# Softmax steps on an even grid of stages, one staging copy per product, and token steps and loads in other places

## The chip, the cores and the metric

The kernel runs on one core of a Trainium2 chip. The metric is device time in microseconds (us), from launch to end. The engines of the core are named as the profile names them: PE (TensorE, matrix products and transposes), DVE (VectorE), ACT (ScalarE), POOL (GpSimd) and SP (SyncE, which issues the DMAs here). Each engine works through its own instructions in the order in which they were written.

## The reference

The program chains three layers over 8 batches of 8 heads, 576 positions and a head width of 64. Keys and values are averaged over groups of 8 positions (72 pooled positions per head), attention is taken over these, and its result, as 4608 tokens of width 512, goes through two feed-forward networks:

```
k_p, v_p = mean of 8 neighbouring positions of k, v
a = softmax(q @ k_p.T / 8) @ v_p            # per batch and head
x = a as (4608, 512)
x = leaky_relu(x @ w_in) @ w_out            # 512 -> 2048 -> 512
xn = x / rms(x) * g
out = (silu(xn @ w_gate) * (xn @ w_val)) @ w_out2   # 512 -> 1536 -> 512
```

All of it is computed to fp32 precision: most operands are split into a high and a low part, and a product takes three matmuls.

## The kernel before

The tokens go through the first network in blocks of 512, j = 0 to 8. Blocks 0 to 4 are computed plainly; blocks 5 to 8 go in two pairs (q = 0, 1) by a scheme with fewer products, and the second network follows in pairs too.

**Stages.** In a plain block PE's work is cut into stages of six matmuls. For each f the order is: two halves of h (`h_half`, product with w_in), then two parts of y for f - 2 (`y_unit`, product with w_out). After the second half of h, `h_high` issues two ACT passes (L101) and `h_low` one DVE subtraction (L619), which make the operand for y. After each stage `attention_point` is called, which issues whatever was put at this point's number. Point 28 is the first of block 1, 92, 156 and 220 are the first of blocks 2, 3 and 4.

**Attention in between.** Attention of batches 0 and 1 is done inside block 0, in an order written out by hand. From batch 2 on `late_attention` puts it at points. A tile is 128 queries of a batch (five tiles, t = 0 to 4; tile number i = 5 b + t, from 10 to 39). `start[i]` is the point at which tile i begins. Its steps are generators, called once per listed point:

- `step_s`: first scores of four heads (PE, L322) and their maximum and subtraction (DVE, L335, L336), then the same for the other four heads one point later, the exponential (ACT, L341) at s + 3, and the normalisation (four DVE instructions, L343 to L346) at s + 4.
- `step_r`: two ACT copies of the leftover columns (L374).
- `step_x`: four transposes on PE (L383), the high part on ACT (L387), the low part on DVE (L389). `step_y` does the same for the leftover columns (L397, L401, L404).
- `step_t`: transposes of the next tile's q (L302) and an ACT copy (L308). `step_kt`: transposes of the next batch's pooled keys and four or eight ACT copies (L294).
- `step_av`: the product with v (four matmuls, L426 and L431). For tokens of blocks 0 to 4 it goes on as high part (ACT, L445) and low part (DVE, L459); for blocks 5 to 8 ACT copies it to a staging tile (L452), which two points later SP stores to DRAM (L454).

Scores, transposes and products of the late batches share two PSUM banks (`bank("att", 2, ...)`), which go round in the order of issue: what takes a bank waits until the one before the last has been read.

**Around the pairs.** In block 4 `first_pair` puts loads and token steps of pair 0 at stage numbers of that block (`put(i, x)` runs ahead of that stage's `attention_point`). Token steps (`token_steps`) make the sums and splits of the pair's inputs on DVE (L1074, L98), ACT and POOL. In the pairs' output stage pieces of six matmuls (L1343) are issued one after another; in the loop over them the loads of the next pair's inputs and the token steps are called at given piece numbers i.

Of the kernel before, what the change touches and what calls it, by code (L numbers as in the profile page):

```python
# [9 lines left out]
F32 = mybir.dt.float32  # L10
# [13 lines left out]
def pooled_attention_then_two_ffns(  # L24
# [13 lines left out]
    nc = tc.nc  # L38
    B, H, S, D = q.shape
    queries = q  # L40
    NT, DM = out.shape
    P = 128
# [9 lines left out]
    N = 512  # L52
# [7 lines left out]
    CHMAX = 320  # L60
# [6 lines left out]
    per = ctx.enter_context(tc.tile_pool(name="per", bufs=1))  # L67
# [12 lines left out]
    def scratch(b, name, early=False):  # L80

        return bank("att", 2, name) if b else bank("ya" if early else "yb", 2, name)
# [21 lines left out]
    def cols(w, f):  # L104
        return w[:, f * W:(f + 1) * W].rearrange("(c p) f -> p c f", p=P)

    def rows(w, f):
        return w[f * P:(f + 1) * P, :]
# [58 lines left out]
    ap = att.__enter__()  # L167
# [5 lines left out]
    for h, sign in ((0, -1), (1, 1)):  # L173
        nc.gpsimd.affine_select(
            out=mask_main[:, h:h + 1], in_=mask_main[:, h:h + 1], compare_op=ALU.is_ge, fill=0.0,
# [4 lines left out]
    for sign, base in ((1, 0), (-1, REST - 1)):  # L180
        nc.gpsimd.affine_select(
            out=group, in_=group, compare_op=ALU.is_ge, fill=0.0, base=base, channel_multiplier=sign,
# [4 lines left out]
        out=mask_rest[:, :, 1], in_=group.rearrange("p d q -> p q d"), axis=AX.X, op=ALU.add  # L187
# [223 lines left out]
    def x_tile(j):  # L411
        if j not in xhl:
            if j == 3:
                xhl[j] = [weight_slot(9 + 2 * c, f"xhl{j}_{c}") for c in range(KC)]
            else:
                t = per.tile([P, 2, KC, N], F32R, tag="xhl", bufs=2, name=f"xhl{j}")
                xhl[j] = [t[:, :, c, :] for c in range(KC)]
        return xhl[j]

    def step_av(b, ci, p):  # L420
        c0, c1, _ = CH[ci]
        n = c1 - c0
        a, ar = at[b, ci]
        pt = scratch(b, f"av{b}_{ci}_{p}")
        for i, (sp, mp) in enumerate(TERMS):
            nc.tensor.matmul(  # L426
                pt[:, :n], vb[b, p][:, sp].rearrange("p h d -> p (h d)"), a[:, p, mp, 0:n],
                start=i == 0, stop=False,
            )
        g, i = divmod(p, 2)  # L430
        nc.tensor.matmul(  # L431
            pt[:, :n], vb[b, NP + g][:, 2 * i:2 * i + 2, :].rearrange("p h d -> p (h d)"), ar[:, g, 0:n],
            start=False, stop=True,
        )
        yield
        spans = []
        t0 = b * S + c0
        while t0 < b * S + c1:
            j = t0 // N
            t1 = min((j + 1) * N, b * S + c1)  # L440
            src = pt[:, t0 - b * S - c0:t1 - b * S - c0]
            if j < PLAIN:
                x = x_tile(j)[p][:, :, t0 - j * N:t1 - j * N]
                spans.append((x, src))
                nc.scalar.activation(out=x[:, HI, :], in_=src, func=AF.Copy)  # L445
            else:
                name = f"xs{b}_{ci}_{p}_{j}"
                if p < 2:
                    x = ap.tile([P, CHMAX], F32, tag="xs", bufs=2, name=name)[:, :t1 - t0]
                else:  # L450
                    x = per.tile([P, N], F32, tag="tg", bufs=3, name=name)[:, :t1 - t0]
                nc.scalar.copy(out=x, in_=src)  # L452
                def store(x=x, j=j, a=t0 - j * N, z=t1 - j * N):
                    nc.sync.dma_start(out=x_dram[j][:, p, a:z], in_=x)  # L454
                at_point.setdefault(point_now[0] + 2, []).append(store)
            t0 = t1
        yield
        for x, src in spans:
            nc.vector.tensor_tensor(out=x[:, LO, :], in0=src, in1=x[:, HI, :].bitcast(F32), op=ALU.subtract)  # L459

    tiles = [(b, t) for b in range(B) for t in range(5)]
# [8 lines left out]
    def go(kind, b, t):  # L470
        if (kind, b, t) not in running:
            running[kind, b, t] = emit[kind](b, t)
        if running[kind, b, t] is not None:
            next(running[kind, b, t], None)
# [33 lines left out]
    def late_attention():  # L508

        def put(point, f):  # L510
            at_point.setdefault(point, []).append(f)

        def stage(kind, b, t, points):
            for point in points:
                put(point, lambda: go(kind, b, t))
            if kind in use:
                def free():
                    live["q" if kind == "t" else "kv"] -= 1
                put(points[0] + 3, free)

        start = {}
        for i in range(FIRST_LATE, len(tiles) + 1):
            start[i] = 34 + round(7.9 * (i - 10))
        for r, point in enumerate((4, 9, 14, 29, 31)):
            stage("kp", 2, r, (point,))
        stage("kt", 2, 0, (28,) * 2)
        stage("kt", 2, 1, (34,) * 2)
        stage("t", 2, 0, (28,) * 2)
        for i in range(FIRST_LATE, len(tiles)):
            b, t = tiles[i]  # L530
            s, after = start[i], start[i + 1]
            stage("s", b, t, (s, s, s + 1, s + 1, s + 3, s + 4))
            stage("r", b, t, (s + 6,))
            stage("x", b, t, (s + 7,) * 3)
            stage("y", b, t, (s + 8,) * 3)
            if i + 1 < len(tiles):
                stage("t", *tiles[i + 1], (s + 6,) * 2)
            if t < 2:
                for k in range(3):
                    stage("vp", b, 3 * t + k, (s + 2 * k,) * 2 + (s + 2 * k + 2,) * 2)  # L540
            if t in (2, 3) and b + 1 < B:
                for k in range(3 if t == 2 else 2):
                    stage("kp", b + 1, 3 * (t - 2) + k, (s + 4 * (t - 2) + 2 * k,))
                stage("kt", b + 1, t - 2, (after + 3,) * 2)
            if t in (1, 4):
                for p in range(NP):
                    stage(f"av{t // 4}", b, p, (after + 2 + p,) * 3)

    point_now = [0]
    first_left = {"V1l5", "T14c"}  # L550
# [27 lines left out]
    for at_, (m, f) in enumerate(needs):  # L578
        src = rows(w_out, f) if m == "o" else cols(w_in, f)
        n = 2 * f + (m == "o")  # L580
# [365 lines left out]
    pairs, kinds = [], []  # L946
# [31 lines left out]
    def pair_loads(q):  # L978

        n = pairs[q][1]  # L980
        xs = [[None] * KC for _ in range(2)]

        def load(z, k):
            x = slot("u", (6, 7, 2, 3)[2 * z + k] if q else 8 + 2 * z + k, f"xst{q}_{z}_{k}").bitcast(F32)
            j = pairs[q][0] // N + z
            nc.sync.dma_start(out=x, in_=x_dram[j][:, 2 * k:2 * k + 2, :])
            for c in range(2):
                xs[z][2 * k + c] = x[:, c, :]

        return xs, [lambda z=z, k=k: load(z, k) for z in range(2) for k in range(2)]  # L990
# [205 lines left out]
    def first_pair(put):  # L1196

        xs, loads = pair_loads(0)
        early, late = token_steps(0, xs, True)
        for i, x in zip((14, 15, 18, 19), loads):  # L1200
            put(i, x)
        for i, x in zip((25, 27, 29, 31, 33, 36, 38, 41), early):
            put(i, x)
        for i, x in zip((58, 59), late):
            put(i, x)
        for i in (34, 36, 39, 41, 42, 44, 46, 48, 50, 52):
            put(i, load_a)
        for i in (53, 55, 57, 59):
            put(i, load_o)
# [260 lines left out]
    n = 0  # L1470
# [10 lines left out]
    for j in range(1, PLAIN):  # L1481
# [3 lines left out]
        def put(i, x):  # L1485
            at_spot.setdefault(i, []).append(x)
# [10 lines left out]
        if last:  # L1497
            first_pair(put)
# [22 lines left out]
    def piece():  # L1521
        if pieces:
            pieces.pop(0)()
# [16 lines left out]
    def tick():  # L1540
        for x in late_side.pop(0) if late_side else ():
            x()

    for q, (_, n) in enumerate(pairs):
# [3 lines left out]
        loads, xs, norm = [], None, []  # L1548
        if more:
            xs, steps = (pair_loads if kinds[q + 1] == 1 else norm_steps)(q + 1)  # L1550
            if kinds[q + 1] == 1:
                loads = steps
# [72 lines left out]
        early, late = token_steps(q + 1, xs, kinds[q] == 1) if more else ([], [])  # L1625
# [11 lines left out]

        for i in range(len(pieces) - (4 if more else 0)):
            if kinds[q] == 1:
                if loads and i in (0, 1, 4, 8):  # L1640
                    loads.pop(0)()
                piece()
                if early + late and (i >= 12 if kinds[q + 1] == 1 else i >= 4 and i % 2 == 0):
                    (early or late).pop(0)()
                for k in (4, 5) if i == 3 else (i // 2 + 4,) if i % 2 and i > 3 else ():
                    if k < F1:
                        second_half(q, k)
                tick()
                continue
            if i % 3 == 0 and early + late:  # L1650
                (early or late).pop(0)()
            piece()
# [42 lines left out]
```

## Time and profile before

| | |
|---|---|
| median of 3 runs | 1814.41 us (1814.34 to 1816.33) |
| profiled execution | 1814.61 us |
| its span, first to last instruction | 1812.9 us |
| PE busy | 1748.3 us, 96% |
| DVE, ACT, POOL busy | 937.2, 720.8, 650.6 us |
| mean granted clock of PE | 0.991 |

The span is counted from the first instruction to the last. Busy time of PE contains modelled ends of matmuls. In a list of waits, `PE sc L322 <- DVE at L389` reads: PE, about to write the tile sc at line 322, stood still until DVE had finished the instruction of line 389 on the tile at. In a timeline a row gives start, duration, engine, line and operation, the tiles, the shapes, and in brackets how long the engine was idle before and what ended that.

### The profile page before, as it was taken

The numbers are of one execution on the slowest core, as the hardware profiler recorded it, in microseconds if no ns is written. First come the engines' busy times: TensorE is split into PE (matmuls) and PEld (weight loads), VectorE is DVE, ScalarE is ACT, GpSimd is POOL, SyncE is SP. The second block draws the span as 40 slices with busy tenths as digits, with TensorE's granted clock in tenths as the row PEclk, the third lists the DMA queues.
The fourth block names the chain that finished last, engine by engine and source line by source line (L and its number), as shares of the span: only waits on it lengthen the run. The fifth ranks groups of instructions, "written<-read, shape, count | busy, mean of one in ns | idle before, by whom it ended". The sixth has DMA issues, their size and how long they took to land.

```text
span 1812.9 us, 24130 instructions
## 1 busy us (share of the span) xinstructions
PE 1748.3 (96%) x8440; PEld 1480.3 (82%) x8440; DVE 937.2 (52%) x1633; ACT 720.8 (40%) x1539; POOL 650.6 (36%) x797
## 2 busy tenths in 40 slices
PE   5899999999999899989999999999999999999999
PEld 4789877777887788867888888899788889988887
DVE  7984445656565454565755345344534444553331
ACT  5664344444454344444553432243232323322220
POOL 5632335535433023443443442154144204513320
PEclk9899999999999999999999999999999999999999
DMA  8543654546666579879996755786775568776562
GB/s 247 191 149 109 231 194 150 162 146 203 192 201 203 165 269 329 302 281 360 313 311 209 238 204 204 227 305 242 247 255 185 188 223 321 253 252 214 187 209 93
DMA packets 214729, 406.36 MB, mean 224 GB/s; under 512 B 58704, under 2 KB 116560, under 8 KB 214096
## 3 DMA queue, kind: packets, MB, share of 16 engines
q1 hardware_dynamic: 214608, 404.82, 66.2%
q8 instruction: 67, 1.10, 0.2%
q14 instruction: 54, 0.44, 0.1%
HBM read 328.21 MB, written 76.55 MB: 223 GB/s over the span
## 4 chain that ended last, share of the span: by engine, by line
PE 79%; DVE 7%; DMA 5%; ACT 3%; issue 3%; POOL 1%; SPq 1%; POOLq 0%; ACTq 0%; DVEq 0%
PE o L1363 16%; PE h L596 8%; PE y L641 8%; PE o L1343 7%; PE yg L1235 6%; PE yv L1235 6%; PE xg L1235 4%; PE xv L1235 4%; PE wg L1235 4%; PE wv L1235 4%; PE yh L1235 3%; PE wh L1235 2%; DMA v<-in_v_dram 2%; PE xh L1235 2%; PE sc L322 2%
## 5 line engine op out<-in xcount | busy, mean ns | idle before, releaser
L1363 PE MATMUL o<-wo,u 128*128 128x512 f32 x1296 | 316.5, 392 | 3.8 <-DMA wo<-wo 3.7
L1363 PEld LDWEIGHTS o<-wo,u 128*128 128x128 f32 x1296 | 243.3, 189 | 53.4 <-DMA wo<-wo 4.7
L596 PE MATMUL h<-xhl,w_i 128*128 128x512 f32 (+1 forms) x996 | 249.9, 393 | 6.9 <-DVE ghl L619 5.5
L596 PEld LDWEIGHTS h<-xhl,w_i 128*128 128x128 f32 x996 | 176.9, 190 | 37.6 <-DVE ghl L619 6.0
L641 PE MATMUL y<-ghl,w_o 128*128 128x256 f32 (+1 forms) x768 | 151.7, 344 | 0.0
L98 POOL TENSOR_TENSOR u<-e2g,u 128x512 fp32r<-128x512 f32 (+1 forms) x25 | 29.6, 1185 | 312.4 <-ACT u L95 312.4
L641 PEld LDWEIGHTS y<-ghl,w_o 128*128 128x128 f32 x768 | 118.7, 192 | 13.2
L619 DVE TENSOR_TENSOR ghl<-h,ghl 128x512 fp32r<-128x512 f32 (+1 forms) x83 | 55.6, 670 | 124.5 <-ACT h L101 124.5
L641 PE MATMUL y<-ghl,wr 128*128 128x512 f32 x384 | 101.8, 405 | 0.0
L1343 PE MATMUL o<-ug,wo 128*128 128x512 f32 x384 | 92.4, 399 | 6.0 <-DMA wo<-wo 3.8
L1343 PE MATMUL o<-u,wo 128*128 128x512 f32 x384 | 96.2, 389 | 0.0
L1343 PEld LDWEIGHTS o<-ug,wo 128*128 128x128 f32 x384 | 73.7, 193 | 23.0 <-issue 4.2
L101 ACT ACTIVATE ghl<-h 128x512 fp32r<-128x512 f32 (+1 forms) x83 | 48.3, 582 | 99.6 <-PE h L596 93.7
L1343 PEld LDWEIGHTS o<-u,wo 128*128 128x128 f32 x384 | 72.1, 188 | 14.9
L1235 PE MATMUL yg<-T,ag 128*128 128x512 f32 (+1 forms) x360 | 84.0, 368 | 0.0
L1235 PE MATMUL yv<-T,av 128*128 128x512 f32 (+1 forms) x360 | 83.8, 368 | 0.0
L1235 PE MATMUL xg<-xa,ag 128*128 128x512 f32 (+1 forms) x360 | 83.8, 367 | 0.0
L1235 PE MATMUL xv<-xa,av 128*128 128x512 f32 (+1 forms) x360 | 83.7, 367 | 0.0
L641 PEld LDWEIGHTS y<-ghl,wr 128*128 128x128 f32 x384 | 70.9, 193 | 12.8
L322 PE MATMUL sc<-kblk,qT 128*128 128x144 f32 x320 | 60.0, 316 | 15.5 <-DVE at L389 9.9
L1235 PEld LDWEIGHTS yg<-T,ag 128*128 128x128 f32 x360 | 66.0, 188 | 10.0 <-DVE e1v L1212 0.6
L1235 PEld LDWEIGHTS yv<-T,av 128*128 128x128 f32 x360 | 66.2, 188 | 9.5
(204 smaller groups left out, 3450.5 us busy)
## 6 DMA issues: line engine op xcount, KB each, us to landing
wo<-wo SPq DMA_DIRECT2D x172, 512.0 KB
ag<-op_g SPq DMA_DIRECT2D x90, 512.0 KB
av<-op_v SPq DMA_DIRECT2D x90, 512.0 KB
wr<-wo SPq DMA_DIRECT2D x32, 512.0 KB
ah<-op_h SPq DMA_DIRECT2D x32, 512.0 KB
k<-in_k_dram SPq DMA_DIRECT2D x40, 256.0 KB
q<-in_q_dram SPq DMA_DIRECT2D x40, 256.0 KB
op_g<-parts_g SPq DMA_DIRECT2D x36, 256.0 KB
```

What stands on the lines that cost most here:

```text
L98: lo_eng.tensor_tensor(out=lo, in0=src, in1=hi.bitcast(F32), op=ALU.subtract)
L101: return nc.scalar.activation(out=out, in_=in_, func=AF.Prelu, scale=scale, alpha=alpha)
L322: nc.tensor.matmul(pt[:, i * n:(i + 1) * n], y[:, p, :], kblk[b % 2][:, p * n:(p + 1) * n], start=True, stop=True,)
L596: nc.tensor.matmul(pt, w[:, sp, c * P:(c + 1) * P], x[c][:, mp, c0:c1], start=c == 0 and i == 0, stop=c == KC - 1 and i == 2,)
L619: nc.vector.tensor_tensor(out=t[:, LO, :], in0=pt, in1=t[:, HI, :].bitcast(F32), op=ALU.subtract)
L641: nc.tensor.matmul(pt, w[:, sp, m * P:(m + 1) * P], g[:, mp, a - c0:a - c0 + n], start=ydone[j, a] == 1 and i == 0 and m % per_bank == 0, ...
L1235: nc.tensor.matmul(pt, wt[:, a, c, sp, :], xt[:, mp, :], start=start and c == 0 and i == 0, stop=c == 1 and i == 2, skip_group_check=not s ...
L1343: nc.tensor.matmul(pt, w[:, sp, m * P:(m + 1) * P], u[:, mp, :], start=f == blocks(q, z)[0] and i == 0, stop=f == blocks(q, z)[-1] and i == 2,
L1363: nc.tensor.matmul(pt, u[:, sp, m * P:(m + 1) * P], w[:, mp, :], start=f == 0 and i == 0, stop=f == F2 - 1 and i == 2,)
```

## The change

- `start[i]` is 33 + 8 (i - 10) in place of 34 + round(7.9 (i - 10)): from 33 to 265 for the tiles, where it was 34 to 263.
- `step_r`, `step_x`, `step_y` and the next tile's `step_t` stand one point sooner after a tile's start, and the products with v one point sooner after its end. Two of batch 2's key steps and one of its transposes move with the first start.
- `step_av` makes one staging copy for a product that crosses two blocks of 512 tokens, and two stores of parts of it, in place of two copies and two stores.
- In block 4 the pair's token steps stand at stages 20 to 46 in place of 25 to 41, and two of its loads a stage sooner.
- In pair 0's output stage the four loads of the next pair's inputs stand at pieces 6, 9, 12 and 15 in place of 0, 1, 4 and 8, and its token steps begin after piece 16 in place of 12.

```diff
-                name = f"xs{b}_{ci}_{p}_{j}"
-                if p < 2:
-                    x = ap.tile([P, CHMAX], F32, tag="xs", bufs=2, name=name)[:, :t1 - t0]
-                else:
-                    x = per.tile([P, N], F32, tag="tg", bufs=3, name=name)[:, :t1 - t0]
-                nc.scalar.copy(out=x, in_=src)
-                def store(x=x, j=j, a=t0 - j * N, z=t1 - j * N):
+                if t0 == b * S + c0:
+                    name = f"xs{b}_{ci}_{p}"
+                    if p < 2:
+                        whole = ap.tile([P, CHMAX], F32, tag="xs", bufs=2, name=name)
+                    else:
+                        whole = per.tile([P, N], F32, tag="tg", bufs=3, name=name)
+                    nc.scalar.copy(out=whole[:, :n], in_=pt[:, :n])
+                def store(x=whole[:, t0 - b * S - c0:t1 - b * S - c0], j=j, a=t0 - j * N, z=t1 - j * N):
...
-            start[i] = 34 + round(7.9 * (i - 10))
-        for r, point in enumerate((4, 9, 14, 29, 31)):
+            start[i] = 33 + 8 * (i - 10)
+        for r, point in enumerate((4, 9, 14, 28, 30)):
...
-        stage("kt", 2, 1, (34,) * 2)
+        stage("kt", 2, 1, (32,) * 2)
...
-            stage("r", b, t, (s + 6,))
-            stage("x", b, t, (s + 7,) * 3)
-            stage("y", b, t, (s + 8,) * 3)
+            stage("r", b, t, (s + 5,))
+            stage("x", b, t, (s + 6,) * 3)
+            stage("y", b, t, (s + 7,) * 3)
             if i + 1 < len(tiles):
-                stage("t", *tiles[i + 1], (s + 6,) * 2)
+                stage("t", *tiles[i + 1], (s + 5,) * 2)
...
-                    stage(f"av{t // 4}", b, p, (after + 2 + p,) * 3)
+                    stage(f"av{t // 4}", b, p, (after + 1 + p,) * 3)
...
-        for i, x in zip((14, 15, 18, 19), loads):
+        for i, x in zip((14, 15, 17, 18), loads):
...
-        for i, x in zip((25, 27, 29, 31, 33, 36, 38, 41), early):
+        for i, x in zip((20, 22, 25, 29, 34, 38, 42, 46), early):
...
-                if loads and i in (0, 1, 4, 8):
+                if loads and i in (6, 9, 12, 15):
...
-                if early + late and (i >= 12 if kinds[q + 1] == 1 else i >= 4 and i % 2 == 0):
+                if early + late and (i >= 16 if kinds[q + 1] == 1 else i >= 4 and i % 2 == 0):
```

From the staging copy on (L452 of before), lines carry a number higher by one in the changed kernel.

Three places show what moves. The first is DVE in tile 0 of batch 6, from its last scores to behind its normalisation; `ghl3_11` is the low part of h for block 3, f = 11. Before:

```order
L336 TENSOR_TENSOR ex6_0_5087<-sc6_0_1_5108,st6_0_5088 128x288
L741 TENSOR_TENSOR raw_g0_0_4939<-raw_g0_0_4939 128x128 x4
L274 TENSOR_TENSOR vb6_0_5134<-vm6_0_5095,vb6_0_5134 128x128
L343 TENSOR_REDUCE st6_0_5088<-ex6_0_5087 128x8
L344 TENSOR_TENSOR st6_0_5088<-st6_0_5088,tiny_67 128x8
L345 RECIPROCAL st6_0_5088<-st6_0_5088 128x8
L346 TENSOR_TENSOR ex6_0_5087<-ex6_0_5087,st6_0_5088 128x576
L274 TENSOR_TENSOR vb6_1_5182<-vm6_1_5141,vb6_1_5182 128x128
L619 TENSOR_TENSOR ghl3_11_0_5200<-h3_11_0_5162,ghl3_11_0_5200 128x512
```

The changed kernel, the same stretch of DVE:

```order
L336 TENSOR_TENSOR ex6_0_5090<-sc6_0_1_5121,st6_0_5091 128x288
L274 TENSOR_TENSOR vb6_0_5139<-vm6_0_5098,vb6_0_5139 128x128
L620 TENSOR_TENSOR ghl3_11_0_5179<-h3_11_0_5151,ghl3_11_0_5179 128x512
L343 TENSOR_REDUCE st6_0_5091<-ex6_0_5090 128x8
L344 TENSOR_TENSOR st6_0_5091<-st6_0_5091,tiny_67 128x8
L345 RECIPROCAL st6_0_5091<-st6_0_5091 128x8
L346 TENSOR_TENSOR ex6_0_5090<-ex6_0_5090,st6_0_5091 128x576
```

The low part of h stood behind the normalisation and now stands ahead of it.

The second place is PE in the same tile, from the second half of h (f = 11) to the transposes of the normalised scores (`xt6_0`). The changed kernel:

```order
L597 MATMUL h3_11_0_5151<-xhl3_3_2772,w_i11_1157 128x512 x3
L426 MATMUL av5_1_3_5183<-at5_1_4800,vb5_3_4542 128x320 x3
L431 MATMUL av5_1_3_5183<-atr5_1_4801,vb5_5_4625 128x320
L642 MATMUL y3_0_0_4518<-ghl3_9_0_5023,wr3_9_4953 128x512 x3
L642 MATMUL y3_0_1_4519<-ghl3_9_0_5023,wr3_9_4953 128x512 x3
L302 MATMUL qt6_1_5216<-ident_63,q6_1_4979 128x128 x4
L642 MATMUL y3_0_2_4520<-ghl3_9_0_5023,wr3_9_4953 128x512 x3
L642 MATMUL y3_0_3_4521<-ghl3_9_0_5023,wr3_9_4953 128x512 x3
L383 MATMUL xt6_0_5236<-ident_63,ex6_0_5090 128x128 x4
```

In this tile PE's rows stand as before, two parts of y between that h and the transposes; what DVE does beside them is in the other order. In a tile that started after a second half of h before, half a further h stood between them too.

The third place is PE at the start of the same tile, from the first scores to the second. Before:

```order
L322 MATMUL sc6_0_0_5084<-kblk0_72,qT6_0_5053 128x144 x2
L596 MATMUL h3_10_0_5070<-xhl3_2_2790,w_i10_1064 128x512 x3
L596 MATMUL h3_10_0_5070<-xhl3_3_2791,w_i10_1064 128x512 x3
L322 MATMUL sc6_0_1_5108<-kblk0_72,qT6_0_5053 128x144 x2
L641 MATMUL y3_0_0_4523<-ghl3_8_0_4983,wr3_8_4895 128x512 x3
```

The changed kernel:

```order
L322 MATMUL sc6_0_0_5087<-kblk0_72,qT6_0_5045 128x144 x2
L642 MATMUL y3_0_0_4518<-ghl3_8_0_4968,wr3_8_4874 128x512 x3
L642 MATMUL y3_0_1_4519<-ghl3_8_0_4968,wr3_8_4874 128x512 x3
L426 MATMUL av5_1_0_5114<-at5_1_4800,vb5_0_4350 128x320 x3
L431 MATMUL av5_1_0_5114<-atr5_1_4801,vb5_4_4583 128x320
L322 MATMUL sc6_0_1_5121<-kblk0_72,qT6_0_5045 128x144 x2
```

A product with v now takes one of the two banks between the first scores and the second.

## Rows read from the trace of the kernel before

**Rows 1.** The page's busy times: us (share of the span) and instructions

```profile
PE 1748.3 (96%) x8440; PEld 1480.3 (82%) x8440; DVE 937.2 (52%) x1633; ACT 720.8 (40%) x1539; POOL 650.6 (36%) x797
```

**Rows 2.** Busy by stretch: us, engines PE PEld DVE ACT POOL, clock, DMA share, GB/s

```profile
176.00:264.00 88.00, 85.95 (x438) 71.37 (x437) 41.53 (x91) 35.79 (x97) 25.62 (x54) 1.00 0.61 219
264.00:400.00 136.00, 128.94 (x648) 104.92 (x647) 79.01 (x180) 58.61 (x150) 67.99 (x111) 0.99 0.53 164
400.00:545.00 145.00, 142.51 (x736) 118.40 (x735) 84.18 (x181) 72.63 (x192) 65.01 (x116) 1.00 0.61 191
545.00:615.00 70.00, 63.44 (x319) 52.31 (x319) 41.35 (x77) 30.00 (x72) 18.35 (x30) 0.98 0.62 194
```

**Rows 3.** PE's waits from 190 to 615 us: total, times, longest

```profile
PE sc L322 <- DVE at L389: 9.4, 12, 2.7
PE xt L383 <- ACT xs L452: 3.1, 2, 2.8
```

**Rows 4.** Busy by stretch again, at the lower clock, columns as in rows 2

```profile
356.80:360.20 3.40, 2.97 (x9) 2.59 (x10) 3.27 (x8) 0.63 (x1) 3.20 (x7) 0.50 0.60 162
...
776.60:783.40 6.80, 5.74 (x14) 4.53 (x15) 0.00 (x0) 0.18 (x1) 1.83 (x4) 0.50 1.04 411
```

**Rows 5.** Timeline near 350 us, tile 1 of batch 4: start, us, engine, line

```profile
349.08 0.69 DVE L619 TENSOR_TENSOR ghl<-h,ghl 128x512 fp32r<-128x512 f32 x1 [3.10 <-ACT h L101]
...
350.84 1.64 PE L596 MATMUL h<-xhl,w_i 128*128 128x512 f32 x6
350.91 0.76 DVE L346 TENSOR_TENSOR ex<-ex,st 128x576 f32<-128x576 f32 x1
```

**Rows 6.** Timeline near 385 us, tile 3 of batch 4, with next batch's keys

```profile
384.23 1.64 PE L596 MATMUL h<-xhl,w_i 128*128 128x512 f32 x6
...
385.04 1.94 POOL L762 TENSOR_TENSOR hr<-w_i 128x256 f32<-128x256 f32 x2
...
385.38 1.02 DVE L346 TENSOR_TENSOR ex<-ex,st 128x576 f32<-128x576 f32 x1
...
386.55 0.63 PE L383 MATMUL xt<-ident,ex 128*128 128x128 f32 x4 [0.68 <-DVE ex L346]
```

**Rows 7.** Timeline from 325 to 338 us, tile 0 of batch 4, with products

```profile
325.28 1.65 PE L641 MATMUL y<-ghl,wr 128*128 128x512 f32 x6
...
327.51 0.46 DVE L336 TENSOR_TENSOR ex<-sc,st 128x288 f32<-128x288 f32 x1
...
331.00 0.60 PE L426 MATMUL av<-at,vb 128*128 128x320 f32 x3
...
336.57 0.76 DVE L346 TENSOR_TENSOR ex<-ex,st 128x576 f32<-128x576 f32 x1
...
337.25 1.64 PE L596 MATMUL h<-xhl,w_i 128*128 128x512 f32 x6
```

**Rows 8.** First pair's output stage: a stretch, a wait of PE, and timeline rows

```profile
760.00:825.00 65.00, 56.46 (x233) 45.01 (x232) 43.25 (x60) 28.48 (x59) 34.19 (x32) 0.95 0.78 273
...
PE yh L1235 <- DVE e6h L1212: 2.6, 1, 2.6
...
765.76 8.09 PE L1343 MATMUL o<-ug,wo 128*128 128x512 f32 x35
...
768.42 0.60 SPq L986 DMA_DIRECT2D xst<-x  x1
...
770.12 1.16 SPq L1186 DMA_DIRECT2D wo<-wo  x2
...
777.66 6.59 PE L1343 MATMUL o<-ug,wo 128*128 128x512 f32 x16 [3.80 <-DMA wo<-wo]
...
787.35 1.37 DVE L98 TENSOR_TENSOR xa<-xst,xa 128x512 fp32r<-128x512 f32 x1 [1.64 <-ACT xa L95]
...
818.01 0.68 DVE L1212 TENSOR_TENSOR e6h<-yh,e1h 128x512 f32<-128x512 f32 x1
```

**Rows 9.** Timeline: one of the token steps' three subtractions in block 4

```profile
580.99 0.68 DVE L1074 TENSOR_TENSOR T<-xst,xst 128x512 f32<-128x512 f32 x1
```

## Prediction

> **What bounds the kernel now.** I read the page first: the line of busy times says that TensorE (PE) works 96% of a span of 1812.9 us, and no other engine more than 52% [rows 1]. So PE is the path, and only two things can change the time: microseconds in which PE stands still, and microseconds in which it has half its clock. Next I cut the part where the change acts into four stretches [rows 2]. From 176 to 615 us (the softmax steps of batches 2 to 7) PE stands still for 2.05 + 7.06 + 2.49 + 6.56 = 18.2 us. Then the list of waits, PE only, for the same part: half of it is scores waiting for the VectorE (DVE) instruction that frees their bank (`sc <- DVE at`, 12 times, longest 2.7), 3.1 is transposes behind ScalarE (ACT) staging copies, longest 2.8 [rows 3]. Behind the longest of each kind a stretch of 3.4 us ran at a granted clock of 0.50, the lower of the two levels (1.2 of 2.4 GHz); the means of 0.99 and 0.98 in rows 2 hold one each. In the one shown PE was busy 2.97 us, half of which is lost: 1.5, so 3.0 in the two [rows 4]. Later PE waits in the first pair's output stage: from 760 to 825 us it stands still 65 - 56.46 = 8.5 us, 3.8 of it at once for weights, and 6.8 us run at the lower clock, 5.74 of them busy, so 2.9 lost [rows 4, 8].
>
> **Part 1, the softmax steps.** Before, a tile starts every 7.9 stages, rounded, so its place against the four-stage pattern (two halves of h, two of y) drifts: tiles 10 to 15 start after the first y, 16 to 24 after the second half of h, 25 to 35 after the first half, 36 to 39 after the second y. In the changed kernel all 30 tiles start after a second half of h (33 + 8k), so tiles 16 to 24 of before stand already where all will stand, and can be measured there.
>
> *What goes.* The four transposes now stand two stages ahead of the next tile's scores and the small transposes one, so the scores no longer find their bank unread. I count all 18.2 us and the 3.0 us of clock as gone and put what comes in their place on the other side.
>
> *What comes, first: the transposes wait for the normalisation.* Four stages after a tile's start, a second half of h has just been computed. DVE takes its instructions in order, and in this place the low part of that h (L619) stands ahead of the normalisation (L343 to L346), as the order in front shows. It can't start until PE has finished h and ACT has done two passes on it. A tile without products, at 346 us, shows the chain: L619 waits for ACT until 349.08 and ends at 349.77, and L346 ends at 350.91 + 0.76 = 351.67 [rows 5]. The stage to which the transposes move (after the second y) ended at 350.84, where the next h starts in that row. Reading the operand took 0.15 us after L346's end elsewhere (386.55 against 385.38 + 1.02) [rows 6]. So PE waits 351.82 - 350.84 = 1.0 us. The one stage of h that the transposes are moved past was the cover, and nothing else is left to cover with; behind them in PE's queue is all further matmul work.
> - Tiles t=1: as this, 1.0 each, six of them: 6.0.
> - Tiles t=3 of five batches: eight ACT copies of the next keys stand ahead of the two passes. L346 ends at 386.40, and the place of the transposes is 384.23: 2.3 us [rows 6]. L346 took 1.02 there instead of 0.76; I take 2.0, five: 10.0.
> - Tiles t=4 with four such copies: estimated between the two, 1.3, five: 6.5.
> - Tiles t=0 and t=2 with products and their DVE low parts (five): L346 ends at 336.57 + 0.76 = 337.33, h starts at 337.25, and one product of 0.60, which now comes ahead of that stage, no longer stands in between: 337.48 - 336.65 = 0.8 each, 4.0 [rows 7]. From batch 4's second half on the products leave no low part on DVE (about 0.4 less): six tiles by 0.3: 1.8. The remaining three without copies or products by 1.0: 3.0.
> Sum 31.3. In the tile at stage 241 the first pair's three subtractions, moved to stage 245, land on DVE between L619 and the normalisation: three by 0.68, 2.1 more with what lies between them [rows 9]. With that 33.4.
>
> *What comes, second: the second scores wait for the first.* Products move a stage sooner, so one takes a bank between the two halves of the scores, and the two banks go round: the second scores now need the bank of the first, which L336 must have read. In the tile at 325 us L336 ends at 327.51 + 0.46 = 327.97, or a little sooner, since the small low part ahead of it (L404) moves away. PE starts y at 325.28; y takes 1.4 (six matmuls at 35 in 8.09 us), the product 0.6, and the small transposes that stood before them are gone, so PE is there by 327.1 [rows 7, 8]: I take 0.8, in eleven tiles (t=0 from batch 3, t=2): 8.8.
>
> These bounds: a wait of the transposes is at least 0.5 and at most 2.6 (2.3 with the longest chain, plus a little); the sum from 24 to 40. The second scores from 0.4 to 1.0: 4 to 11.
>
> *Clock.* Waits of 2.7 and 2.8 us brought a stretch at half clock [rows 3, 4]; one of 2.6 didn't: the mean clock of 0.95 from 760 to 825 us is explained by the 6.8 us behind the wait for weights alone (6.8 by 0.5 of 65 is 0.05) [rows 4, 8]. Of the new waits only the one with the subtractions (3.1) is above: 1.5.
>
> Softmax part: 33.4 + 8.8 + 1.5 - 18.2 - 3.0 = +22.5 us.
>
> **Part 2, one staging copy.** Twelve 256-column copies replace 24 pieces of batches 5, 6 and 7, whose second piece waited for a store to free its slot. Its gain on PE is the 3.1 us of transposes behind `xs` [rows 3], in the 18.2 already; ACT itself has room (40%) [rows 1]. If the single copies should still wait, up to 3.1 comes back, and the 1.5 of clock behind the longest.
>
> **Part 3, first pair's token steps in the last block.** The same instructions on ACT and DVE, over more stages; cost nothing but the 2.1 above. Loads a stage earlier: what they read was stored some 20 stages before. The last products and their stores come a stage later than before, with PE on its own last four h and y stages: 0, bounded by -1 and +2.
>
> **Part 4, the loads in the first pair's output stage.** Three loads of 512 KB were issued from 768.42 on, around the two weight loads at 770.12 for which PE then stood 3.80 us, until 777.66 [rows 8]. Moved to pieces 6, 9, 12 and 15, they come after those weights in SyncE's (SP's) queue, and one of them, not three, shares the engines with them: I take the 3.8 and the 2.9 of clock as gone. Against that, the token steps start four pieces later (24 matmuls, at 35 in 8.09 us 5.5 us), and DVE was busy almost without a break from 787.35 to 818.69, the addition that PE waited for last [rows 8]. Part of the DVE work falls into the gap now left before them, part of the shift is covered by the 4.7 us that PE waited there anyhow (8.5 less 3.8): I take 2.0 lost, between 0 and 5.5. If all waits there go, -11.4; if the weights wait as before, +5.5. Taken: -3.8 - 2.9 + 2.0 = -4.7.
>
> **Sum.** 1814.61 (the profiled execution, 1.7 of it outside its span) + 22.5 - 4.7 = 1832.4; the median lies 0.2 below that execution: 1832.2.
>
> **A rule of the Trainium skill.** L346 took 0.76 us in two of the tiles above and 1.02 in the third, where a GpSimd instruction of 1.94 us ran beside it [rows 5 to 7]. The Trainium skill, SBUF — State Buffer, section "Who interferes with whom", says that a DVE instruction with two SBUF inputs and a GpSimd instruction that reads SBUF shut each other out. The trace agrees with 0.26 us. If every tile met it, 30 by 0.26 would add 7.8, which lies in the range.
>
> **Rivals.**
> *The transposes don't wait (faster).* If the normalisation were through when PE comes, only 8.8 of new waits would stand against 18.2 + 3.0 + 4.7: 1814.4 - 17.1 = 1797. For it: from 400 to 545 us, where the tiles start a stage earlier in the pattern, PE stands still 2.5 us in 145 [rows 2]. Against it: there the normalisation is ahead of the low part on DVE, and after the change never. It decides from a mean of 0.57 us per tile: below that, the time falls. 12%.
> *About even.* The new waits three quarters of what I read (31.7) and part 4 at its best: 31.7 + 1.5 - 21.2 - 11.4 = +0.6, so 1815. 8%.
> *The clock falls at each long wait.* Five tiles wait some 2 us, less than any wait that halved the clock here, and less than the 2.6 that did not. If each does, 5 by 1.5 = 7.5: 1840. TensorE: Matmul & The Clock Gate, section "HAM oscillation — how this bites in real kernels", of the Trainium skill tells of a kernel whose clock fell at every tile's wait, and paid each time; of before's trace only the two longest waits in the softmax part agree. 8%.
> *Part 4 only moves its wait.* The weights wait for later loads, or PE finds the token steps unready at the second pair: the softmax part's +22.5 stands alone or with up to 5.5 more, so 1837 to 1842. For it: DVE's unbroken chain. 12%.
> *My own reading, part 4 as taken:* 60%, 1820 to 1844.
>
> **How the numbers follow.** A measurement of this kernel tells 0.2% (3.6 us) from no change. Slower by more: 60 + 8 + 12 = 80, less 2 for the lower edge of my own range: 78%. Faster by more: 12, plus 2 from the even case: 14%. Within: 8%. Range: from 1812, which leaves the faster case out, to 1848.
>
> **What would show it.** In the new profile: PE's list has `xt <- DVE ex L346` as its longest row, near 30 waits and 25 to 40 us, `sc <- DVE at` near nothing, and `sc <- DVE ex L336` some 8 us. The L343 rows stand right behind an L620 each time. The 3.8 at `o <- DMA wo` is gone, and the stretch after 780 us is nearer its own pace. ACT's waits for `x <- xs` become few. I am wrong if `xt` waits stay under 0.5 us each, that is if L620 and the normalisation end before the second y does.

## The result and the profile after

The changed kernel takes 1832.61 us (median of 4 runs, 1832.07 to 1833.75), the kernel before 1814.38 beside it (1813.86 to 1816.33). The ratio is 1.0099, with an interval from 1.0082 to 1.0117: 18.2 us slower, where 1832.2 was forecast. The profiled execution of the changed kernel has a span of 1830.4 us. Two terms of the sum were wrong by nearly the same amount in opposite directions, so the terms are looked at one by one.

The page's line of busy times, after:

```profile
PE 1750.5 (96%) x8440; PEld 1478.9 (81%) x8440; DVE 934.7 (51%) x1633; ACT 718.1 (39%) x1527; POOL 649.1 (35%) x797
```

The same instructions on PE, 12 fewer on ACT [rows 1]: the time went into waiting and clock. By stretches of the softmax steps, columns as in [rows 2]:

```profile
176.00:264.00 88.00, 82.63 (x422) 67.98 (x421) 39.59 (x87) 33.93 (x92) 24.21 (x51) 1.00 0.57 208
264.00:400.00 136.00, 125.18 (x624) 102.21 (x623) 74.95 (x174) 56.64 (x145) 64.61 (x109) 0.97 0.53 167
400.00:560.00 160.00, 150.84 (x769) 123.89 (x768) 84.36 (x189) 72.63 (x187) 66.45 (x118) 1.00 0.57 176
560.00:632.00 72.00, 65.53 (x327) 53.15 (x326) 40.50 (x76) 31.74 (x74) 18.86 (x29) 0.98 0.61 190
```

PE stands still for 5.37 + 10.82 + 9.16 + 6.47 = 31.8 us, where it was 18.2 [rows 2]. PE's waits from 190 to 640 us (total, times, longest) say for what:

```profile
PE xt L383 <- DVE ex L346: 24.1, 24, 2.9
PE sc L322 <- DVE ex L336: 4.6, 6, 2.5
PE sc L322 <- ACT xs L453: 1.4, 3, 0.5
PE xt L383 <- ACT xs L453: 0.6, 1, 0.6
```

The wait of scores for the low part of the transposes (L389), 9.4 us before [rows 3], is gone, and both forecast waits have come. In the timeline, the tile that answers to [rows 5], batch 4, t = 1:

```profile
351.96 0.69 ACT L341 ACTIVATE ex<-ex 128x576 f32<-128x576 f32 x1 [0.68 <-DVE ex L336]
...
355.93 0.69 DVE L620 TENSOR_TENSOR ghl<-h,ghl 128x512 fp32r<-128x512 f32 x1 [2.60 <-ACT h L101]
...
356.33 1.64 PE L642 MATMUL y<-ghl,wr 128*128 128x512 f32 x6
...
357.76 0.76 DVE L346 TENSOR_TENSOR ex<-ex,st 128x576 f32<-128x576 f32 x1
...
358.66 0.63 PE L383 MATMUL xt<-ident,ex 128*128 128x128 f32 x4 [0.69 <-DVE ex L346]
```

The exponential (L341) is through at 352.65. DVE then stands still for 2.60 us with the low part of h (L620) at the head of its queue, the normalisation follows, and PE, through with y at 357.97, stands still until 358.66. A tile t = 3 with eight ACT copies for the next keys, as in [rows 6]:

```profile
467.84 1.64 PE L642 MATMUL y<-ghl,wr 128*128 128x512 f32 x6
468.18 0.69 DVE L620 TENSOR_TENSOR ghl<-h,ghl 128x512 fp32r<-128x512 f32 x1 [5.18 <-ACT h L101]
...
470.00 0.76 DVE L346 TENSOR_TENSOR ex<-ex,st 128x576 f32<-128x576 f32 x1
...
470.91 0.63 PE L383 MATMUL xt<-ident,ex 128*128 128x128 f32 x4 [1.42 <-DVE ex L346]
```

The copies hold ACT's two passes on h back, so L620 starts 0.34 us after that y starts, not 0.40 ahead of it, and the wait is 1.42. The second scores of tile 0 of batch 4 [rows 7] wait behind a product:

```profile
333.14 0.60 PE L426 MATMUL av<-at,vb 128*128 128x320 f32 x3
...
333.67 0.46 DVE L336 TENSOR_TENSOR ex<-sc,st 128x288 f32<-128x288 f32 x1
...
334.27 0.73 PE L322 MATMUL sc<-kblk,qT 128*128 128x144 f32 x4 [0.38 <-DVE ex L336]
```

And the first pair's output stage, a stretch that begins and ends with the same work as in [rows 8]:

```profile
777.20:842.90 65.70, 56.98 (x233) 44.69 (x232) 43.37 (x60) 28.49 (x59) 34.51 (x32) 0.92 0.77 281
```

PE stands still for 8.7 us in it, where it was 8.5. Its longest waits, and those for weights:

```profile
PE xh L1236 <- ACT e1h L1279: 4.7, 1, 4.7
PE yh L1236 <- DVE e6h L1213: 2.3, 1, 2.3
PE o L1344 <- DMA wo<-wo: 0.7, 2, 0.4
```

The 3.80 us for weights fell to 0.7, and in its place PE waits 4.66 us for ACT's copy e1h, which was on no list before. The timeline shows what that copy was queued behind:

```profile
809.92 0.69 DVE L1075 TENSOR_TENSOR T<-xst,xst 128x512 f32<-128x512 f32 x1 [2.44 <-DMA xst<-x]
...
826.15 1.75 DVE L1075 TENSOR_TENSOR xst<-xst,T 128x512 f32<-128x512 f32 x1
...
827.94 1.15 ACT L95 ACTIVATE xb<-xst 128x512 fp32r<-128x512 f32 x2 [1.02 <-DVE xst L1075]
...
829.54 0.56 ACT L1279 COPY e1h<-xh 128x512 f32<-128x512 f32 x1
830.16 2.93 PE L1236 MATMUL xh<-xa,ah 128*128 128x512 f32 x6 [4.66 <-ACT e1h L1279]
```

DVE's first sum waits 2.44 us for a later load, the last sums end at 827.9, ACT's split xb waits for them, and the copy that PE needs stands behind that split.

Matching the starts of equal work in both traces gives the difference along the program: 0.3 us less at the start of block 1, 3.0 more at that of block 2, 9.1 of block 3, 14.7 of block 4, 17.6 behind block 4; then 9.2 at the sixtieth group of six output matmuls (piece 27 of the loop, counted from 0), and 17.9 behind the second pair's first products.

### The profile page after: what moved, and what is told of

It is laid out like the page before. It is cut to its first block, busy times and chain, and to the rows that moved or that the text cites. A ratio compares the mean times of both kernels' runs of the same rounds, so it can differ in the third digit from the quotient of the medians.

```text
span 1830.4 us, 24096 instructions
## 1 busy us (share of the span) xinstructions
PE 1750.5 (96%) x8440; PEld 1478.9 (81%) x8440; DVE 934.7 (51%) x1633; ACT 718.1 (39%) x1527; POOL 649.1 (35%) x797
## 4 chain that ended last, share of the span: by engine, by line
PE 80%; DVE 9%; ACT 4%; DMA 3%; issue 2%; POOL 1%; SPq 1%; ACTq 0%; POOLq 0%; DVEq 0%
PE o L1364 15%; PE h L597 9%; PE o L1344 7%; PE y L642 7%; PE yg L1236 6%; PE yv L1236 6%; PE xg L1236 4%; PE xv L1236 4%; PE wg L1236 4%; PE wv L1236 4%; PE yh L1236 3%; PE wh L1236 2%; PE xh L1236 2%; PE sc L322 2%; DMA wo<-wo 1%
## 5 line engine op out<-in xcount | busy, mean ns | idle before, releaser
L620 DVE TENSOR_TENSOR ghl<-h,ghl 128x512 fp32r<-128x512 f32 (+1 forms) x83 | 55.7, 671 | 164.3 <-ACT h L101 164.1
L1236 PEld LDWEIGHTS xv<-xa,av 128*128 128x128 f32 x360 | 66.1, 188 | 9.6
L1236 PEld LDWEIGHTS xg<-xa,ag 128*128 128x128 f32 x360 | 66.1, 188 | 9.4
```

Of the source, the lines that this page charges most:

```text
L620: nc.vector.tensor_tensor(out=t[:, LO, :], in0=pt, in1=t[:, HI, :].bitcast(F32), op=ALU.subtract)
L1236: nc.tensor.matmul(pt, wt[:, a, c, sp, :], xt[:, mp, :], start=start and c == 0 and i == 0, stop=c == 1 and i == 2, skip_group_check=not s ...
```

## Experiments

Each is the changed or the old kernel with the edit shown. The kernel before took 1815.21 us beside the normalisation on the changed kernel, the transposes, both output moves and the loads alone; 1814.05 beside the normalisation on the kernel before, the staging copy and the old and middle places; 1813.58 beside the products, the token steps and the last. Differences are taken within the same group. "Behind block 4" is the difference in start times from the profiled kernel before.

**Normalisation a stage sooner, on the changed kernel (norm_sooner).**

```diff
-            stage("s", b, t, (s, s, s + 1, s + 1, s + 3, s + 4))
+            stage("s", b, t, (s, s, s + 1, s + 1, s + 2, s + 3))
```

> The changed kernel with the exponential at s + 2 and the normalisation at s + 3, a stage sooner each; PE's order is unchanged, only DVE and ACT take the normalisation ahead of the low part of h. Theory (the transposes wait because the normalisation stands behind that low part): PE's waits xt <- L346 fall from 24.1 us to under 5, the time by about 20 to 1812 us (1807 to 1818). Rival (the chain scores, exponential, normalisation is itself too long for transposes at s + 6): the waits stay above 15 us and the time above 1826 us.

1796.55 us, ratio 0.9906 (0.9885 to 0.9927): 18.7 below before. Behind block 4 it stands 18.1 us ahead of before and 35.7 ahead of the changed kernel. PE's waits from 190 to 650 us:

```profile
PE sc L322 <- DVE ex L336: 3.7, 6, 1.6
PE sc L322 <- ACT xs L453: 1.4, 3, 0.5
PE xt L383 <- ACT xs L453: 1.4, 1, 1.4
PE av L426 <- DVE atr L404: 1.3, 1, 1.3
```

The 24 waits behind L346 are gone. A tile near 300 us, same columns as the timelines above:

```profile
297.32 0.92 DVE L346 TENSOR_TENSOR ex<-ex,st 128x576 f32<-128x576 f32 x1
...
300.05 1.64 PE L642 MATMUL y<-ghl,w_o 128*128 128x512 f32 x6
300.35 0.69 DVE L620 TENSOR_TENSOR ghl<-h,ghl 128x512 fp32r<-128x512 f32 x1 [2.11 <-ACT h L101]
301.52 0.60 PE L383 MATMUL xt<-ident,ex 128*128 128x128 f32 x4
```

L346 now ends at 298.24, ahead of L620, with 3.3 us to spare. In the changed kernel the exponential was done at 352.65 in the tile shown, and DVE stood still before L620: the data were there, and the order held the normalisation back. That DVE's order made the waits is shown.

**Transposes back a stage, on the new grid.**

```diff
-            stage("r", b, t, (s + 5,))
+            stage("r", b, t, (s + 6,))
...
-            stage("x", b, t, (s + 6,) * 3)
-            stage("y", b, t, (s + 7,) * 3)
+            stage("x", b, t, (s + 7,) * 3)
+            stage("y", b, t, (s + 8,) * 3)
...
-                stage("t", *tiles[i + 1], (s + 5,) * 2)
+                stage("t", *tiles[i + 1], (s + 6,) * 2)
```

> The changed kernel with the leftover copies, both transposes and the next tile's q back one stage (s + 6, s + 7, s + 8, s + 6), all else as changed. Theory: one stage of h is cover again, xt <- L346 falls to about 6 us, scores wait some 2 us for the low part of the transposes, the second scores keep their 5 us: about 1818 us (1813 to 1822). Rival (it is the products with v a stage sooner, or the even grid itself, that costs): no more than 5 us come back, 1827 us or more.

1822.78 us, 1.0045 (1.0029 to 1.0061). The waits change places (190 to 640 us):

```profile
PE sc L322 <- DVE at L389: 10.6, 7, 3.2
PE xt L383 <- DVE ex L346: 4.3, 6, 1.6
```

The transposes' waits fall from 24.1 to 4.3 us, and the scores' wait for the low part of the transposes comes back. So the sooner transposes do remove the old wait and do cost more than it: 10.3 of the 17.6 us behind block 4. Without them the changed kernel is still 7.3 us behind before there.

**Normalisation sooner, on the kernel before.** The first experiment's edit, on the old grid.

> The kernel before with only the normalisation (exponential part at s+2, scaling at s+3) one stage sooner. Theory: there the transposes stood late enough and TensorE waited for a scores bank that the copies of the small transposes free late; a sooner normalisation doesn't touch that, so 1814, between 1810 and 1816, and the waits of scores for the copies (12, 9.4 us in all) stay. Rival: the normalisation's place alone is worth what norm_sooner gained (35.7 us against the changed kernel, 18 against before): 1796 to 1800.

1810.58 us, 0.998 (0.9969 to 0.9991): within the expected range, far from 18. The waits of scores that the expectation puts down to the small transposes are those for the low part of the large ones, `at` of L389; they stay (12, 7.5 us in all, longest 1.4 where it was 2.7). The normalisation's place is worth 3.5 us there and some 36 on the changed kernel. How much of that kernel's gain hangs on the sooner transposes, and how much on the grid and the products, no run separates; the staging copy has its share (next but one).

**Products back a stage, on the changed kernel.**

```diff
-                    stage(f"av{t // 4}", b, p, (after + 1 + p,) * 3)
+                    stage(f"av{t // 4}", b, p, (after + (1 if i == len(tiles) - 1 else 2) + p,) * 3)
```

> The changed kernel with the products with v back at the stage where they stood relative to the next tile's start (only the very last tile's stay, as there is no later stage). Theory: the second scores waited for the bank of the first only because a product took a bank between them, so the six waits of scores for the exponential part (4.6 us, the longest 2.55 with a stretch at half clock behind it, 1.7 us) go: 6 us less, 1826.5, between 1824 and 1829. Rival: the product only changes its place against the transposes, covers nothing or brings waits of the products for the copies of the small transposes: 1831 to 1834.

1822.26 us, 1.0045 (1.0027 to 1.0063). This gained 9.5 us, not 6. The scores' waits for L336 and for staging copies (6.0 us) are gone, and so are the stretches at half clock behind 312 and 367 us (1.7 us lost in each); waits of products behind L336 (2.0, 2) and of transposes behind L460 (1.7, 5) came. But the tile with the subtractions now waits 3.14 us, and the stretch at half clock that stood behind it is longer, 6.8 us in place of 3.4:

```profile
582.50:589.30 6.80, 5.96 (x17) 4.83 (x18) 2.64 (x5) 2.20 (x6) 0.61 (x1) 0.50 0.23 60
```

It costs 3.0, so the clock gives back 5.1 - 3.0 = 2.1. Up to the end of block 4 PE stands still 6.2 us less, in 13 fewer waits, and 9.9 us are won. The second scores' waits went as expected. The expectation left out the waits for staging copies (1.4), the transposes' waits (2.1 less) and what a wait costs beside its listed time (below).

**One staging copy, on the kernel before.** The first part of the diff alone.

> The kernel before with only the single staging copy of each product (part 2). The prediction's term: 0 by itself, at most the 3.1 us of transposes behind staging copies and 1.5 us of clock won: 1810 to 1814.5. Rival: the store of the first piece now waits for the copy of both, and the stores land late for what loads them, or the larger copies hold ScalarE longer ahead of the h passes: 1816 or more, with new waits of h or of the loads of these products.

1807.26 us, 0.9965 (0.9954 to 0.9976). Nothing on PE waits for `xs` any more (4.7 us before, 3.1 of it transposes), 4.9 us are won behind block 4, and 2.4 more in the first pair's output stage. Part 2 is a gain by itself. The rival, later stores, is refuted.

**Token steps in block 4 back, on the changed kernel.**

```diff
-        for i, x in zip((20, 22, 25, 29, 34, 38, 42, 46), early):
+        for i, x in zip((25, 27, 29, 31, 33, 36, 38, 41), early):
```

> The changed kernel with the first pair's token steps in the last block back at their old stages. Theory (the prediction's 2.1 us): the three subtractions stood ahead of one normalisation; without them that tile's wait of 2.89 us falls to some 0.7 and the half clock behind it (1.7 us) may go: 1828.5 to 1830.5. Rival: the subtractions were not what made that wait, or other ones take it up (steps bunched on VectorE in the same stages as before): 1832 to 1834, with the long wait still there.

1837.2 us, 1.0128 (1.0106 to 1.015): not faster, rather 5 us slower than the changed kernel, though the two intervals meet. The tile near 592 us, free of the subtractions, waits 1.55 us and not 2.89, but others take the work up. The profiled execution, the fastest of the four at 1832.29, shows 2.4 us of the loss at the end of block 4. DVE near 623 us:

```profile
621.47 0.69 DVE L620 TENSOR_TENSOR ghl<-h,ghl 128x512 fp32r<-128x512 f32 x1 [2.87 <-ACT h L101]
622.53 1.37 DVE L98 TENSOR_TENSOR T<-T,T 128x512 fp32r<-128x512 f32 x1 [0.37 <-ACT T L95]
623.82 0.68 DVE L1075 TENSOR_TENSOR xst<-xst,T 128x512 f32<-128x512 f32 x1
624.42 0.74 DVE L343 TENSOR_REDUCE st<-ex 128x8 f32<-128x576 f32 x1
```

Here two instructions of the token steps stand between L620 and the normalisation, and the tile waits 3.02. The rival held: in both places the steps fall on some tile's way, and the spread costs less than the bunch.

**Both moves of the output stage, on the kernel before.**

```diff
-                if loads and i in (0, 1, 4, 8):
+                if loads and i in (6, 9, 12, 15):
...
-                if early + late and (i >= 12 if kinds[q + 1] == 1 else i >= 4 and i % 2 == 0):
+                if early + late and (i >= 16 if kinds[q + 1] == 1 else i >= 4 and i % 2 == 0):
```

> The kernel before with part 4 alone: loads at pieces 6, 9, 12, 15 and token steps from 16. The new trace says: 8 us are won until the end of the output stage and as much is lost at the second pair's first products, so 1814.8 us (1812 to 1818). The prediction's own term said -4.7: 1809.7 us.

1816.21 us, 1.0005 (0.9992 to 1.0019). The stretch wins 7.9 us up to piece 27 and then loses 10.2, with the same wait of 4.7 for e1h in it. My term of -4.7 is refuted on its own ground.

**The loads alone, on the kernel before.** Loads at pieces 3, 6, 9 and 11, token steps from 12 as they were.

> The kernel before with the loads at pieces 3, 6, 9, 11 and the token steps where they were (from 12). If the loss at the second pair comes from the token steps' later start, this keeps the win at the weights without the loss: 1808 us (1805 to 1811). If it comes from the loads landing late, DVE waits for the last load here as well and PE waits behind it: 1813 us or more.

1815.06 us, 1.0003 (0.999 to 1.0016). 5.7 us are won by piece 12; 4.2 of them are given back by piece 26, the rest at the second pair's first products. PE's waits in the stage:

```profile
PE o L1343 <- DVE ug L98: 2.6, 1, 2.6
PE yh L1235 <- DVE e6h L1212: 2.6, 1, 2.6
PE o L1343 <- DMA wo<-wo: 1.7, 2, 0.9
PE o L1343 <- POOL ug L98: 1.4, 1, 1.4
```

Even with the steps where they were, the win turns into waits for splits (`ug`) that stand behind token steps on DVE and POOL. When the steps begin isn't the whole cause. PE's waits in this stage sum to 8.5 us in the kernel before, 8.7 in the changed one and 9.1 in this and the last experiment: they change place more than size. That the work which has to get through beside the output matmuls sets the sum is likely, not shown.

**Normalisation sooner, old or middle places in the output stage.** The first experiment's kernel with loads at (0, 1, 4, 8) and steps from 12, and with loads at (3, 5, 7, 9) and steps from 10.

> The changed kernel with the normalisation one stage sooner (norm_sooner, 1796.55 us) and with the loads and token steps of the first pair's output stage back where they stood before the change. Theory: moving them was worth nothing net (what the weights' wait gave back, 6 to 8 us by piece 27, was lost again at the second pair's first products), so undoing it leaves norm_sooner's time, 1796, between 1792 and 1799; in the trace the 3.8 us wait of the output matmuls for weights comes back near piece 12 and the 4.66 us wait of the xh transposes goes. Rival, the prediction's own term: moving them was worth 4.7 us, so undoing it costs that: 1801, and the 3.8 us comes back without another wait going.

> norm_sooner with the loads ahead of pieces 3, 5, 7 and 9 and a token step behind every piece from 10 on. Theory: the win is lost because VectorE's chain of token steps ends too late, so it has to start sooner: loads done by some 780 us, chain begun six pieces (some 8 us) sooner than in the changed kernel, no wait above 1 us at the second pair's first products, and no weights' wait: 5 to 8 us below norm_sooner, 1789 to 1792. Rival: loads that close to the weight loads hold these up again, or the token steps wait for their loads at the head of VectorE's queue and hold up the u splits that TensorE wants: 1796 to 1800.

1794.44 us (0.9888, 0.9871 to 0.9904) and 1793.59 (0.9884, 0.987 to 0.9899). Undoing the move costs nothing, as the first theory said, and the weights' wait of 3.1 is back. Against before, the middle places win 4.8 us up to piece 12, stand 3.5 behind at piece 26 after two waits of 2.7 for `ug`, and end 0.6 ahead, as the wait for e6h is gone: my 5 to 8 missed. All waits of the stage sum to 7.9 and 7.6 us.

**All of it: normalisation sooner, products back, loads at 3, 5, 7, 9, steps spread.** The first two edits and the places of the loads are as above; this line is new:

```diff
-                if early + late and (i >= 16 if kinds[q + 1] == 1 else i >= 4 and i % 2 == 0):
+                if early + late and (i >= 9 and i % 3 != 2 if kinds[q + 1] == 1 else i >= 4 and i % 2 == 0):
```

> The changed kernel with the normalisation one stage sooner, the products one stage back, the first pair's loads ahead of pieces 3, 5, 7 and 9, and the token steps two behind every three pieces from 9 on. Theory: the 3.7 us of second scores go, and the u splits, which waited 2.7 us each behind a step behind every piece, get through between spread steps: 1793.6 - 3.7 - 3 = 1787, between 1784 and 1790. Rival: TensorE waits some 7.6 us in this output stage whatever the places of the steps (7.9 with the old ones, 7.6 with loads from piece 3), because the steps' work has to come between the u splits anyhow: 1789 to 1793, the e6h wait longer because the last step comes later.

1789.81 us (1787.68 to 1791.75), ratio 0.9869 (0.9851 to 0.9887), 23.8 us below before and the best of all. The longest wait left in the softmax part (180 to 632 us):

```profile
PE qt L302 <- issue: 1.2, 1, 1.2
```

4 us in all are left there. In the output stage 3.3 us were won up to the last pieces, and 1.8 given back (e6h, 2.9). The time lies where the ranges of the two expectations meet (1789 to 1790). Against the middle places, 4.7 us came up to the end of block 4, with the second scores' waits gone; of the 3 us for the spread, 0.9 came in the output stage, whose waits sum to 7.2, near what the rival said.

## Why the forecast came out, step by step

**The mechanism of part 1 was right.** Every tile's transposes wait for the normalisation, and its place behind the low part of h is the cause (first experiment). By kinds of tile the trace shows for t = 1 0.69 (1.29 once; I took 1.0), for t = 3 1.91, 2.28 and three of 1.42 (I took 2.0), for t = 4 0.69 to 1.56 (1.3), for t = 0 and 2 0.08 to 0.75 (0.3 to 0.8), 2.89 with the subtractions. The sum over 30 tiles is 26.8 us, not 33.4; the second scores make 6.1 in ten, not 8.8 in eleven.

**What failed in it: two measures in one sum.** I took my new waits from start to start, and subtracted the old ones as the list counts them. A matmul group starts before the one ahead of it has drained, by the ends that the profile models: in the sooner normalisation's timeline y runs from 300.05 to 301.69 and the transposes start at 301.52. Behind a wait that overlap of 0.17 us is lost on top of the listed idle time: the 0.69 above costs 0.86. Between the sooner normalisation and the changed kernel the same is seen in sum: from 219.5 us (217.2 in the sooner one) to behind block 4, the same instructions, 26 fewer waits, 23.4 us less idle time, 5.1 less for clock, but 33.4 less elapsed; 4.9 over 26 waits is 0.19 each. So in one measure (an estimate, 0.17 for each wait) the new waits cost 26.8 + 5.1 = 31.9 and 6.1 + 1.7 = 7.8, close to what I gave, and the old ones, 30 of them, 18.2 + 5.1, not 18.2. The term too small was what the change removes.

**Clock, too small.** I gave 1.5 for one stretch. There were three, and PE was busy through each, so 1.7 lost each, 5.1. With it the softmax part is 31.9 + 7.8 + 5.1 - 23.3 - 3.0 = +18.5 by terms, +17.6 measured, +22.5 forecast; the last 0.9 I can't assign.

**Part 2** was 0 beyond the 4.6 us counted with the removed waits and clock; alone it gave 4.9 in that part, so the step held in size. Not in its terms: the clock near 592 us fell all the same, and 1.6 us of other waits for `xs` went in its place. Another 2.4 in the output stage I didn't have. **Part 3**: the 2.1 is right for that tile (2.89 against the 0.69 of others of its kind), but the cost of 0 for the rest left out what the old places would have cost on the new grid: by the experiment the spread saves rather than costs.

**Part 4 failed**: -4.7 forecast, +0.4 measured. The weights' wait and the clock behind it did go (-8.3 up to the sixtieth group); the step that failed is the 2.0 for token steps that start later. I bounded it by the shift on DVE, at most 5.5, and looked for the end of its chain at e6h alone. The chain crosses to ACT: a split there waits for DVE's last sums, and the copy that PE needs is behind it. This wait stands in each of the kernels run with both moves (loads up to piece 15, steps after 16), and in none with steps that begin sooner; no run has the one move's late place without the other's, so their shares stay open. From the sixtieth group on it all cost 8.7, with 10.2 us at half clock (2.9 of it). The rival "part 4 only moves its wait" is what happened, and its price stood in the forecast.

So the errors were -4.9 in the softmax part and +5.1 in part 4, and the sum hit by their cancelling, which is luck: by its own terms it was 5 us off twice. The rule on DVE and GpSimd, which I priced at up to 7.8 us for all tiles, counted little in the mean; the grouped row for the normalisation, from 176 to 640 us (instructions, total, mean in ns), is

```profile
L346 DVE TENSOR_TENSOR ex<-ex,st 128x576 f32<-128x576 f32 x30 | 23.4, 780 | 1.0
```

## What to carry to other kernels

Before moving a consumer sooner, find what stands ahead of its producer in that engine's queue, and move the producer past it in the same change: here the change, with only the consumer sooner, left the softmax part 17.6 us behind (7.3 with the transposes put back), and the same change with the producer sooner too left it 18.1 ahead, 4.9 of which the staging copy gives by itself on the old grid. Price waits that come and waits that go in the same measure, from start to start of the work. A wait taken out of a stage pays only if the next-latest chain, followed through every engine that it crosses, has room.

## What the runs showed of the hardware

**The same wait may or may not bring half clock.** Behind 2.28 us at 311.95 the changed kernel's clock fell; columns as in [rows 4]:

```profile
312.50:315.90 3.40, 3.40 (x11) 2.57 (x10) 0.69 (x1) 1.14 (x3) 0.29 (x2) 0.51 1.08 344
```

With the token steps back, the same place has a wait of 2.27 at 311.96, and no fall:

```profile
312.00:315.40 3.40, 3.40 (x18) 2.85 (x19) 1.40 (x3) 1.66 (x5) 0.73 (x3) 1.00 1.03 331
```

With one staging copy, the clock held behind the longest wait of scores (2.69), and fell behind one of 1.31 (first PE's rows in the timeline, then the two stretches):

```profile
356.98 0.76 PE L322 MATMUL sc<-kblk,qT 128*128 128x144 f32 x4 [2.69 <-DVE at L389]
...
590.50 0.76 PE L322 MATMUL sc<-kblk,qT 128*128 128x144 f32 x4 [1.31 <-DVE at L389]
...
356.90:360.30 3.40, 2.96 (x15) 2.32 (x16) 3.27 (x9) 0.63 (x1) 3.24 (x7) 1.00 0.52 145
591.70:595.10 3.40, 3.40 (x12) 2.84 (x11) 3.19 (x7) 0.00 (x0) 0.00 (x0) 0.50 0.11 41
```

My threshold between 2.6 and 2.7 us was no threshold: the length of one wait doesn't decide. TensorE: Matmul & The Clock Gate, section "HAM oscillation — how this bites in real kernels", of the Trainium skill tells of a kernel that pays at every tile, behind waits of some 3 to 5 us; here the 40 waits of the softmax part were at most 2.9 us, and 3 of them paid.

**One small DVE instruction took 2.60 us.** It stands at the head of the DVE chain behind which the changed kernel's second scores waited longest (2.55 at 367.19):

```profile
358.55 0.42 DVE L274 TENSOR_TENSOR vb<-vm,vb 32x256 fp32r<-32x256 f32 x1
...
360.73 2.60 DVE L274 TENSOR_TENSOR vb<-vm,vb 32x256 fp32r<-32x256 f32 x1
...
360.94 1.42 POOL L763 TENSOR_TENSOR hr<-w_i 128x256 f32<-128x256 f32 x2
```

The same instruction took 0.42 two microseconds sooner; the second time GpSimd instructions ran beside it. SBUF — State Buffer, section "Who interferes with whom", of the Trainium skill says that the two engines lock each other out of a shared port; the trace agrees with 2.2 us here. That the lock is the cause was not tested.
